# A retention and SwiGLU kernel whose instruction list is made anew: row tiles for the state products, stores on a second queue

## The chip, the cores and the metric

The kernel runs on one core of a Trainium2 chip. Its engines work side by side, each through its own instructions in order: TensorE (PE) multiplies matrices, VectorE (DVE), ScalarE (ACT) and GpSimd (POOL) do elementwise work, and SyncE (SP) issues DMA transfers. The metric is the device time of one execution in microseconds (us), as the median of several runs. Smaller is better.

## The reference

Two parts are chained. The first is a retention recurrence over 4 batches, 8 heads, 768 positions and 64 channels:

```python
gamma = 1.0 - 2.0 ** (-5.0 - np.arange(H))
for t in range(S):
    state = gamma * state + np.einsum('bhd,bhe->bhde', k[:, :, t], v[:, :, t])
    y[:, :, t] = scale * np.einsum('bhd,bhde->bhe', q[:, :, t], state)
```

The second takes y as 3072 rows (tokens) of 512 numbers and applies a normalised feed-forward block with an inner width of 1536:

```python
xn = x / np.sqrt(np.mean(x * x, axis=-1, keepdims=True) + 1e-06) * rms_g
g = xn @ w_gate
out = (g * (1.0 / (1.0 + np.exp(-g))) * (xn @ w_val)) @ w_out
```

## The kernel before, in words

The 768 positions are cut into six chunks of 128 (index c, 0 to 5). A tile is one chunk of one batch, (c, b), 128 tokens. For each tile the scores inside the chunk are computed by a matrix product, masked, and multiplied with v; what came before the chunk is held in a state per batch and head and enters as a second product, q times state. All matrix products are in bf16, with f32 sums in PSUM, which has eight banks.

There are no loops in the program's flow. One long string, ORDER, lists every step by a short name, and the kernel emits the steps in this order. Each engine then works through its own steps in the order of the list, and waits between engines and for buffers are put in from what each step reads and writes. A word of the list reads name.numbers/banks@engine: "/53" gives the PSUM bank or banks that the step writes to, "@D", "@A", "@P", "@S" the engine (DVE, ACT, POOL, SP). A bank may be written anew only when the last reader of its old contents is done. The steps that matter:

- Lq, Lk, Lv load rows of q, k, v; Cq and V scale them to bf16; tq and tk transpose them by DMA on SP (in chunks 0 and 1: Tq and Tk on PE, with the copies Eq and Ek); D scales k by decay.
- A (L401) makes the scores of one or two tiles, heads in pairs: with 64 rows each, two products run in two row tiles of the array. M0 and M1 (L423) mask them on DVE, two instructions a tile.
- Y (L438, L442) multiplies the masked scores of a tile with v, eight matmuls, and adds q times state, four matmuls with 128 rows and 128 columns over two heads each, all in one bank.
- Z (L414) makes the q times state products of a pair of tiles (b, b+1) ahead of that, each head by itself: 16 matmuls of 64 rows and 64 columns in row tiles, even heads in one bank and odd heads in another. After it Y.c.b.2 (L433) adds only the eight score products.
- S (ACT, L455) squares and sums a tile's rows, R (POOL, L465, L467) makes the factor of the normalisation, N (DVE, L479) applies it. After Z the tile's even and odd heads lie in two banks: S and N then take two instructions each (L452, L476), and R adds the two sums first (L464).
- X and XE transpose the normalised rows for the feed-forward part: XE by DMA on SP from chunk 2 on, before that X on PE and XE as a copy.
- K, U and B bring the state from one chunk to the next: products on PE (L525), addition on DVE (L534), cast on POOL (L541).
- g and v (L549) are the gate and value products, four matmuls for each block of 128 of the inner width; s (ACT, L560) is the silu, h (DVE, L568) the product of the two.
- d (L575) is the down-projection of a tile, twelve matmuls of 512 columns, sometimes in two parts. e (L597) does it for the last tile in three column pieces. o copies the result from PSUM (ACT or DVE), and st stores it to memory (L588).
- H (L234) are matmuls without use for the result, in places where PE would wait in the head.

The list before has one Z, for the pair (4,2) and (4,3), and all stores on SP. The buffers in SBUF are rings; six result buffers (o_sb), six scaled q, ten k, and so on, so a load or a copy may also wait for an old buffer's readers.

Of the kernel before, what the change touches and what calls it, by code (L numbers as in the profile page):

```python
# [17 lines left out]
Lk.0.2@S H.4/4 yd causal Lv.0.2@S>causal yt rms.1@S ident Ck.0.2@A Lq.0.0@P H.8/1 Lq.0.1@P Lq.0.2@P Tk.0.2/7 H.2/5  # L18
Lk.0.0@P Tq.0.1/0 vd Tq.0.0/4 Ek.0.2@D Lk.0.1@P Tq.0.2/1 Lk.0.3@P G/7 V.0.2@D Eq.0.1@D Tk.0.0/0 Tk.0.1/6 Eq.0.2@D
Eq.0.0@D iota Lq.0.3@P A.0.2/31 Lv.0.1@P mk0 Lv.0.0@P Lv.0.3@P Ek.0.0@D mk1 GE@A wg.0.2 M1.0.2 wv.0.2 H.2/4 M0.0.2  # L20
Ek.0.1@A A.0.0/5270 D.0.2@P M1.0.1 Tk.0.3/6 Y.0.2/1 Tq.0.3/0 M0.0.1 H.2/4 tab Lk.1.1@P M1.0.0 M0.0.0 S.0.2 Ek.0.3@A
J.0.0/4 J.0.1/7 R.0.2 Y.0.1/2 Eq.0.3@A S.0.1 H.1/6 H.3/0 H.1/5 D.0.0@D Y.0.0/3 N.0.2 J.0.3/5 D.0.1@D wv.2.4 R.0.1
X.0.2/6 N.0.1 S.0.0 wg.2.4 A.0.3/41 R.0.0 X.0.1/0 XE.0.2@A wg.4.6 D.0.3@D M0.0.3 XE.0.1@A g.0.0.2.2.3/2 K.0.2.2/5
K.0.0.2/6 M1.0.3 U.0.2.2@A s.0.0.2.2.3 N.0.0 v.0.0.2.2.3/7 g.0.0.2.1.2/0 h.0.0.2.2.3 Y.0.3/5 Lq.1.0@P wv.4.6 X.0.0/3
U.0.0.2@A S.0.3 wg.6.9 Tk.1.1/4 v.0.0.2.1.2/2 XE.0.0@D s.0.0.2.1.2 h.0.0.2.1.2 g.0.0.2.0.1/6 R.0.3 wv.6.9 Ek.1.1@A
v.0.3.4.0.3/3 v.0.2.3.0.3/4 N.0.3 g.0.3.4.0.3/0 Lk.1.2@P s.0.0.2.0.1 X.0.3/6 v.0.0.2.0.1/5 XE.0.3@A Lk.1.0@P B.0.0
wg.9.12 s.0.3.4.0.3 Lq.1.1@P g.0.5.6.0.3/1 g.0.2.3.0.3/7 h.0.3.4.0.3 s.0.2.3.0.3 Lq.1.2@P h.0.2.3.0.3 g.0.4.5.0.3/0
wv.9.12 h.0.0.2.0.1 s.0.4.5.0.3 v.0.0.4.3.4/2 g.0.0.4.3.4/7 v.0.4.5.0.3/3 mc.1@P s.0.5.6.0.3 s.0.0.4.3.4 h.0.0.4.3.4
wo.0.4 v.0.5.6.0.3/4 h.0.5.6.0.3 D.1.1@P Lv.1.1@P h.0.4.5.0.3 Lv.1.0@P g.0.8.9.0.4/7 g.0.6.7.0.4/0 mc.0@D s.0.8.9.0.4
v.0.4.6.3.4/4 g.0.4.6.3.4/5 s.0.4.6.3.4 v.0.8.9.0.4/6 D.1.0@D D.1.2@P wo.4.8 s.0.6.7.0.4 Tk.1.2/2 Ek.1.2@D Tq.1.0/5  # L30
g.0.7.8.0.4/1 Eq.1.0@D h.0.8.9.0.4 v.0.6.7.0.4/7 h.0.4.6.3.4 wo.8.12 v.0.7.8.0.4/3 s.0.7.8.0.4 h.0.6.7.0.4
g.0.11.12.0.4/5 s.0.11.12.0.4 Tk.1.0/7 h.0.7.8.0.4 Tq.1.1/0 Lv.1.2@P Lq.1.3@P Tq.1.2/3 Eq.1.1@D B.0.1 Eq.1.2@D
g.0.9.10.0.4/4 s.0.9.10.0.4 B.0.2 g.0.10.11.0.4/2 s.0.10.11.0.4 Ek.1.0@D A.1.0/3710 M1.1.1 A.1.2/46 v.0.10.11.0.4/2
v.0.11.12.0.4/0 M0.1.2 M0.1.1 v.0.9.10.0.4/5 M0.1.0 Lv.2.0@S d.0.0.0.4/1 M1.1.0 M1.1.2 h.0.9.10.0.4 Y.1.1/3
d.0.3.0.4/6 Lk.2.3@P h.0.11.12.0.4 Y.1.0/4 S.1.1 Lk.1.3@P R.1.1 h.0.10.11.0.4 S.1.0 N.1.1 d.0.1.0.4/0 R.1.0
d.0.2.0.4/5 N.1.0 X.1.1/3 d.0.2.4.8 d.0.0.4.8 Lv.1.3@P d.0.3.4.8 X.1.0/7 d.0.3.8.12 XE.1.0@A Y.1.2/2 Tq.1.3/7
d.0.0.8.12 S.1.2 d.0.1.4.8 Lq.2.0@S XE.1.1@D o.0.0@A Eq.1.3@D o.0.3@A R.1.2 N.1.2 Tk.1.3/1 d.0.2.8.12 X.1.2/3 Ek.1.3@A
Lk.2.2@P D.1.3@D Lq.2.1@S A.1.3/17 XE.1.2@A M1.1.3 K.1.0/4 K.1.2.2/6 K.1.1/2 B.0.3 M0.1.3 Lq.2.2@S tk.2.2 Lk.2.0@P
g.1.0.1.0.3/3 v.1.2.3.0.3/7 U.1.1@D Y.1.3/1 s.1.0.1.0.3 g.1.1.2.0.3/3 S.1.3 Lk.2.1@P g.1.3.4.0.3/2 o.0.2@A R.1.3
U.1.2.2@D d.0.1.8.12 Cq.2.1@P s.1.3.4.0.3 U.1.0@D g.1.2.3.0.3/2 v.1.0.1.0.3/5 N.1.3 Lq.3.1@S s.1.1.2.0.3 X.1.3/3  # L40
h.1.0.1.0.3 tk.2.0 v.1.3.4.0.3/1 Lk.3.1@P tq.2.1 v.1.1.2.0.3/5 B.1.2 XE.1.3@D h.1.3.4.0.3 s.1.2.3.0.3 h.1.2.3.0.3
# [595 lines left out]
```

## Time and profile before

| | |
|---|---|
| median of 3 runs | 232.84 us (232.34 to 233.55) |
| the profiled execution | 231.99 us |
| its span, first to last instruction | 230.3 us |
| granted TensorE clock | 1.000 |
| PE busy | 224.7 us (98%) |
| DVE, ACT, POOL busy | 127.8, 84.2, 105.7 us |
| HBM read, written | 28.31 MB, 6.29 MB |

The profile is of one execution. Its times are in us from the first instruction. A row of a timeline gives the start, the length, the engine, the line, the operation with output and inputs, how many instructions were put together, and in brackets how long the engine was idle before and what released it. Matmuls overlap a little at their ends, so the length of a PE step is best read from its start to the start of the next one. Rows of groups give the total time and the mean in nanoseconds behind the bar.

### The profile page before, as it was taken

The page shows a single profiled execution, that of the slowest core. Times are in us where ns is not written, and L with a number is a line of the kernel's source. Part 1 is how long each engine was busy: PE and PEld are TensorE (multiplying, and loading weights), DVE is VectorE, ACT ScalarE, POOL GpSimd, SP SyncE. Part 2 cuts the span into 40 slices and gives each one's busy share as a digit, 9 for nine tenths or more (in the row PEclk, how much of TensorE's full clock was granted, in tenths as well). Part 3 has the DMA queues.
Part 4 walks back from the last instruction along what each step waited for, and adds up shares of the span by engine and source line. Part 5 has one row for each costly group of instructions (what it writes and reads, how often), then busy time and mean ns, then how long its engine had stood idle before and what let it go on. Part 6 is the DMA issues. An engine that isn't in the chain of part 4 may idle for free.

```text
span 230.3 us, 4745 instructions
## 1 busy us (share of the span) xinstructions
PE 224.7 (98%) x1849; PEld 118.9 (52%) x1849; DVE 127.8 (55%) x232; ACT 84.2 (37%) x190; POOL 105.7 (46%) x177
## 2 busy tenths in 40 slices
PE   8889999999999999999999999999999999999994
PEld 2568755556564554445544445554554444444552
DVE  5896397936654876477660538756664325432200
ACT  6776524225423340434410435561354124222021
POOL 8979999327879435536269801338040000000000
PEclk9999999999999999999999999999999999999999
DMA  6999999999999957999999999674116200000142
GB/s 130 162 175 134 187 176 191 199 192 134 141 180 164 156 110 180 215 187 228 184 84 288 177 179 271 132 85 90 49 23 198 101 0 0 0 16 35 45 181 92
DMA packets 105352, 31.51 MB, mean 137 GB/s; under 512 B 94449, under 2 KB 102385, under 8 KB 105330
## 3 DMA queue, kind: packets, MB, share of 16 engines
q0 software_dynamic: 40112, 9.70, 45.5%
q1 hardware_dynamic: 65218, 21.51, 43.7%
q8 instruction: 14, 0.23, 0.4%
q14 instruction: 8, 0.07, 0.1%
HBM read 28.31 MB, written 6.29 MB: 150 GB/s over the span
## 4 chain that ended last, share of the span: by engine, by line
PE 93%; DVE 2%; DMA 2%; POOL 1%; issue 0%; ACT 0%; POOLq 0%; DVEq 0%
PE v_ps L549 27%; PE g_ps L549 27%; PE o_ps L575 26%; PE a_ps L401 2%; PE y_ps L438 2%; DMA qb<-in_q_dram 2%; PE y_ps L442 2%; PE kv_ps L525 1%; PE o_ps L597 1%; DVE am L423 1%; PE t_ps L369 1%; PE xt_ps L492 1%; DVE kd L514 1%; PE t_ps L364 1%; POOL qb L307 1%; PE g_row_ps L290 0%
## 5 line engine op out<-in xcount | busy, mean ns | idle before, releaser
L568 DVE TENSOR_TENSOR hT<-sg,v_ps 128x512 bf16<-128x512 bf16 (+2 forms) x76 | 48.0, 656 | 55.4 <-PE v_ps L549 40.2
L560 ACT ACTIVATE sg<-g_ps 128x512 bf16<-128x512 f32 (+2 forms) x76 | 42.3, 575 | 93.6 <-PE g_ps L549 85.2
L549 PE MATMUL g_ps<-xnT,wg_b 128*128 128x512 bf16 (+2 forms) x344 | 71.1, 344 | 0.0
L549 PE MATMUL v_ps<-xnT,wv_b 128*128 128x512 bf16 (+2 forms) x344 | 71.0, 344 | 0.0
L575 PE MATMUL o_ps<-wo_b,hT 128*128 128x512 bf16 x276 | 63.4, 379 | 0.0
L549 PEld LDWEIGHTS <-wg_b 128*128 128x128 bf16 x344 | 30.6, 98 | 29.9 <-issue 0.3
L549 PEld LDWEIGHTS <-wv_b 128*128 128x128 bf16 x344 | 30.5, 98 | 29.1 <-DVE hT L568 0.2
L575 PEld LDWEIGHTS <-hT 128*128 128x128 bf16 x276 | 26.3, 98 | 29.7
L465 POOL TENSOR_SCALAR ms<-ssq 128x1 f32<-128x1 f32 x24 | 4.5, 188 | 42.0 <-ACT xsq L455 41.1
L423 DVE TENSOR_TENSOR am<-a_ps,causal 128x512 bf16<-128x512 f32 x32 | 20.1, 684 | 3.2 <-PE a_ps L401 3.2
L479 DVE SCALAR_TENSOR_TENSOR xn<-y_ps,rstd,g_bc 128x512 bf16<-128x512 f32 x22 | 16.4, 749 | 9.8 <-POOL rstd L467 8.0
L541 POOL CAST st_b<-st_f 64x256 bf16<-64x256 f32 x40 | 18.1, 452 | 5.4 <-DVE st_f L534 4.1
L455 ACT ACTIVATE xsq<-y_ps 128x512 f32<-128x512 f32 x22 | 13.1, 598 | 15.6 <-PE y_ps L442 14.1
L309 POOL DMA_DIRECT2D kb<-in_k_dram x20 | 18.4, 921 | 0.0
L140 ACT COPY o_sb<-o_ps 128x512 f32<-128x512 f32 (+1 forms) x15 | 8.4, 568 | 24.0 <-PE o_ps L575 23.7
L337 POOL TENSOR_TENSOR qb<-qf,ydec 128x512 bf16<-128x512 f32 x13 | 13.9, 1069 | 5.0 <-DMA qf<-in_q_dram 2.3
L467 POOL TENSOR_TENSOR rstd<-ms,mhalf 128x1 f32<-128x1 f32 x24 | 13.3, 555 | 2.0
L140 DVE COPY o_sb<-o_ps 128x512 f32<-128x512 f32 (+2 forms) x11 | 6.7, 622 | 13.3 <-PE o_ps L575 7.6
L356 POOL TENSOR_TENSOR vp<-vf,vdec 128x512 bf16<-128x512 f32 x9 | 9.3, 1046 | 3.7 <-DMA vf<-in_v_dram 3.5
L423 DVE TENSOR_TENSOR am<-a_ps,mask 128x512 bf16<-128x512 f32 x16 | 9.9, 682 | 1.6 <-PE a_ps L401 1.5
L438 PEld LDWEIGHTS <-am 128*128 128x128 bf16 x176 | 7.7, 98 | 3.5
L234 PE MATMUL hot_ps<-one 128*128 128x512 bf16 x23 | 7.9, 491 | 1.1 <-DVE one L147 1.1
(96 smaller groups left out, 158.9 us busy)
## 6 DMA issues: line engine op xcount, KB each, us to landing
out_dram<-o_sb SPq DMA_DIRECT2D x23, 256.0 KB, 2.4
vf<-in_v_dram SPq DMA_DIRECT2D x17, 256.0 KB, 4.1
qf<-in_q_dram SPq DMA_DIRECT2D x16, 256.0 KB, 4.5
kb<-in_k_dram POOLq DMA_DIRECT2D x23, 128.0 KB, 5.4
wo_b<-in_moe_w_out_dram POOLq DMA_DIRECT2D x3, 512.0 KB, 10.3
qb<-in_q_dram POOLq DMA_DIRECT2D x8, 128.0 KB, 5.6
vp<-in_v_dram POOLq DMA_DIRECT2D x7, 128.0 KB, 6.2
wg_b<-in_moe_w_gate_dram POOLq DMA_DIRECT2D x3, 256.0 KB, 5.8
```

What stands on the lines that cost most here:

```text
L140: return (e.copy if e is ACT else e.tensor_copy)(out, in_)
L309: i = done[n, c, b] = e.dma_start(out=x, in_=rows[n][b, c])
L337: e.tensor_tensor(out=u["qb"], in0=u["qf"], in1=ydec[:, c, :, None].to_broadcast([128, H, D]), op=ALU.mult)
L423: return DVE.tensor_tensor(out=u["am"][:, i], in0=u["a"][i], in1=m, op=ALU.mult)
L455: return ACT.activation(xsq, flat(u["y"]), AF.Square, accum_out=u["ssq"])
L467: return POOL.tensor_tensor(out=u["rstd"], in0=ms, in1=mhalf, op=ALU.pow)
L479: return DVE.scalar_tensor_tensor(out=u["xn"], in0=flat(u["y"]), scalar=u["rstd"], in1=g_bc, op0=ALU.mult, op1=ALU.mult)
L541: POOL.tensor_copy(st_b[b][r, :, i * 64:i * 64 + 64], st_f[b // 2][r, b % 2])
L549: r = nc.tensor.matmul(p[:, (n - n0) * m:(n - n0 + 1) * m], W[w][0][:, s, n * 128:(n + 1) * 128], xnT[c][:, s, b0 * C:b1 * C], start=s == ...
L560: return ACT.activation(sg[:, :cols], done["wg", c, n0, b0][:, :cols], AF.Silu)
L568: return DVE.tensor_tensor(out=hT[c][:, n0:n1, b0 * C:b1 * C], in0=sg, in1=p, op=ALU.mult)
L575: nc.tensor.matmul(o_ps[c, b], hT[c][:, n, b * C:(b + 1) * C], wo_b[:, n, :], start=n == 0, stop=n == NFF - 1)
```

## The change

Only the string ORDER differs. The first 202 words are the same steps on the same engines in the same order, up to the last masks before the first down-projection; the banks in them are numbered anew. From there on:

- five more pairs get a Z and the short Y: (2,0), (3,0), (4,0), (5,2) and (5,0), with banks of their own;
- 15 stores are issued by ACT instead of SP;
- the order of all steps, the banks, and the engine of some 30 copies and scalings (o, V, Cq) are new.

The core of the diff, the first words, the beginning of the new part, and two places of the later list:

```diff
 ...
-Lk.0.2@S H.4/4 yd causal Lv.0.2@S>causal yt rms.1@S ident Ck.0.2@A Lq.0.0@P H.8/1 Lq.0.1@P Lq.0.2@P Tk.0.2/7 H.2/5
+Lk.0.2@S H.4/0 yd causal Lv.0.2@S yt rms.1@S ident Ck.0.2@A Lq.0.0@P H.8/1 Lq.0.1@P Lq.0.2@P Tk.0.2/0 H.2/1 Lk.0.0@P
 ...
-K.0.0.2/6 M1.0.3 U.0.2.2@A s.0.0.2.2.3 N.0.0 v.0.0.2.2.3/7 g.0.0.2.1.2/0 h.0.0.2.2.3 Y.0.3/5 Lq.1.0@P wv.4.6 X.0.0/3
+M1.0.3 U.0.2.2@A s.0.0.2.2.3 N.0.0 v.0.0.2.2.3/5 g.0.0.2.1.2/0 h.0.0.2.2.3 Y.0.3/3 Lq.1.0@P wv.4.6 X.0.0/5 U.0.0.2@A
 ...
-v.0.3.4.0.3/3 v.0.2.3.0.3/4 N.0.3 g.0.3.4.0.3/0 Lk.1.2@P s.0.0.2.0.1 X.0.3/6 v.0.0.2.0.1/5 XE.0.3@A Lk.1.0@P B.0.0
+v.0.2.3.0.3/6 N.0.3 g.0.3.4.0.3/3 Lk.1.2@P s.0.0.2.0.1 X.0.3/5 v.0.0.2.0.1/2 XE.0.3@A Lk.1.0@P B.0.0 wg.9.12
 ...
-v.0.4.6.3.4/4 g.0.4.6.3.4/5 s.0.4.6.3.4 v.0.8.9.0.4/6 D.1.0@D D.1.2@P wo.4.8 s.0.6.7.0.4 Tk.1.2/2 Ek.1.2@D Tq.1.0/5
-g.0.7.8.0.4/1 Eq.1.0@D h.0.8.9.0.4 v.0.6.7.0.4/7 h.0.4.6.3.4 wo.8.12 v.0.7.8.0.4/3 s.0.7.8.0.4 h.0.6.7.0.4
+v.0.4.6.3.4/3 g.0.4.6.3.4/6 s.0.4.6.3.4 v.0.8.9.0.4/0 D.1.0@D D.1.2@P wo.4.8 s.0.6.7.0.4 Tk.1.2/6 Ek.1.2@D Tq.1.0/2
+g.0.7.8.0.4/4 Eq.1.0@D h.0.8.9.0.4 v.0.6.7.0.4/6 h.0.4.6.3.4 wo.8.12 v.0.7.8.0.4/0 s.0.7.8.0.4 h.0.6.7.0.4
 ...
+o.2.1@D s.3.8.9.0.4 h.3.8.9.0.4 s.3.0.1.0.4 tq.4.0 A.4.0/3205 Lv.4.2@S h.3.0.1.0.4 Z.4.0/64 M1.4.1 M1.4.0 Lv.4.1@S
+v.3.2.3.0.4/7 st.1.0@A Lv.4.3@S Cq.4.3@P M0.4.0 g.3.2.3.0.4/5 g.3.11.12.0.4/2 g.3.7.8.0.4/3 V.4.0@P M0.4.1 tq.4.3
+Lk.4.2@P s.3.10.11.0.4 tk.4.2 Lq.4.2@S s.3.2.3.0.4 V.4.3@D st.1.3@S Lk.4.3@P Y.4.0.2 s.3.11.12.0.4 v.3.10.11.0.4/2
+S.4.0 V.4.2@A Cq.4.2@D V.4.1@D h.3.2.3.0.4 d.2.2.0.12/5 h.3.10.11.0.4 R.4.0 N.4.0 tk.4.3 Lq.5.2@S tq.4.2 A.4.2/2701
 ...
-o.5.1@A st.4.2@S o.5.3.1@D d.5.2.0.12/0 st.5.3.2@S st.5.1@S st.5.3.1@S e.5.3.0/1 o.5.2@A st.5.2@S o.5.3.0@A st.5.3.0@S
+o.5.0@A o.5.1@A st.5.0@A o.5.2@A st.4.0@S st.5.1@S o.5.3.1@A st.5.2@S e.5.3.0/5 st.5.3.2@A o.5.3.0@A st.5.3.0@A
+st.5.3.1@S
```

134 lines of the change are left out of this document (65 added, 69 removed).

## The prediction

> **What bounds the kernel now.** I read the page first, then the waits of TensorE's own queue, then the timelines of TensorE (PE) and VectorE (DVE) side by side.
>
> ```profile
> span 230.3 us, 4745 instructions
> PE 224.7 (98%) x1849; PEld 118.9 (52%) x1849; DVE 127.8 (55%) x232; ACT 84.2 (37%) x190; POOL 105.7 (46%) x177
> PE 93%; DVE 2%; DMA 2%; POOL 1%; issue 0%; ACT 0%; POOLq 0%; DVEq 0%
> ```
>
> ```profile
> PE hot_ps L234 <- DVE one L147: 1.1, 1, 1.1
> PE t_ps L364 <- DMA qb<-in_q_dram: 0.5, 1, 0.5
> PE xt_ps L492 <- DVE xn L479: 0.4, 1, 0.4
> PE t_ps L364 <- DVE am L423: 0.2, 1, 0.2
> ```
>
> PE is the bound. The four waits above are all that it has, 2.2 us, and the last of them lies at 17 us. From there to its last product the matmuls stand shoulder to shoulder. So the change can win only matmul time, and can lose wherever a new order or a new bank makes PE wait. There is little to gain and much room to lose.
>
> **The state products as row tiles.** Five pairs are new (pair 4.2 had it already). Rows from PE's timeline; a step lasts from its start to the start of the next:
>
> ```profile
> 78.33 0.39 PE L442 MATMUL y_ps<-st_b,qT 128*128 128x128 bf16 x4
> 78.64 0.44 PE L525 MATMUL kv_ps<-vp,kb 128*64 128x64 bf16 x16
> 79.02 0.62 PE L401 MATMUL a_ps<-qT,kT 64*128 64x128 bf16 x16
> ...
> 82.40 0.39 PE L442 MATMUL y_ps<-st_b,qT 128*128 128x128 bf16 x4
> 82.63 0.40 PE L438 MATMUL y_ps<-vp,am 128*128 128x64 bf16 x8
> ...
> 148.67 0.41 PE L414 MATMUL y_ps<-st_b,qT 64*128 64x64 bf16 x16
> 149.01 1.04 PE L549 MATMUL v_ps<-xnT,wv_b 128*128 128x512 bf16 x4
> ```
>
> The state part of one tile is 0.23 us (82.40 to 82.63), of a pair 0.46; the 16 row tiles of a pair take 0.34 (148.67 to 149.01). That saves 0.12 us a pair, 0.6 for five. Going from whole-array matmuls to tiles costs something too: after the four of 78.33 (0.23) the kv products begin at 78.64, 0.08 late, while kv to a_ps has no such gap. Counted through both lists there are 18 such entries before and 20 after, so 0.16 goes back. Net: -0.4 us. [...] The pair measured here shows 0.46 against 0.34, a factor of 1.35, and I take the row. [...]
>
> What the row tiles add elsewhere: each of ten tiles gets two squares, two accumulator reads, two normalisations and an addition.
>
> ```profile
> L455 ACT ACTIVATE xsq<-y_ps 128x512 f32<-128x512 f32 x22 | 13.1, 598 | 15.6 <-PE y_ps L442 14.1 <-PE y_ps L438 1.3
> L455 ACT ACTIVATION_READ_ACCUMULATOR xsq<-y_ps 128x1 f32 x22 | 4.4, 199 | 0.0
> L452 ACT ACTIVATE xsq<-y_ps 128x256 f32<-128x256 f32 x4 | 1.5, 392 | 0.0
> L452 ACT ACTIVATION_READ_ACCUMULATOR xsq<-y_ps 128x1 f32 x4 | 0.9, 219 | 0.0
> L476 DVE SCALAR_TENSOR_TENSOR xn<-y_ps,rstd,g_bc 128x256 bf16<-128x256 f32 x4 | 1.8, 480 | 2.1 <-POOL rstd L467 2.1
> L464 POOL TENSOR_TENSOR ssq<-ssq 128x1 f32<-128x1 f32 x2 | 0.4, 192 | 7.1 <-ACT xsq L452 7.1
> ```
>
> ACT: 2 x (392 + 219) - (598 + 199) = 0.43 us a tile; POOL 0.19; DVE 2 x 480 less one whole normalisation (0.74 in a row below) = 0.22. The way from a tile's scores to its transposed rows gets 0.84 us longer. Cover: by PE's steps in the new list 7 to 10 us of matmuls stand between the last scores of a chunk and the first gate product that reads them. If that cover were gone, PE would pay up to 0.84 once a chunk, for four chunks; I take 0.
>
> **The banks of the head.** The list's first 202 words are the same, but the numbers behind the slashes (PSUM banks) are not. A matmul that takes a bank waits until the last reader of what lay in it is done. So each new pair of reader and taker is to be checked at the times of the old run. Most pass. These do not:
>
> ```profile
> 18.62 0.74 DVE L479 SCALAR_TENSOR_TENSOR xn<-y_ps,rstd,g_bc 128x512 bf16<-128x512 f32 x1
> 19.28 0.41 DVE L568 TENSOR_TENSOR hT<-sg,v_ps 128x256 bf16<-128x256 bf16 x1
> ...
> 21.92 0.75 DVE L479 SCALAR_TENSOR_TENSOR xn<-y_ps,rstd,g_bc 128x512 bf16<-128x512 f32 x1 [0.74 <-POOL rstd L467]
> ```
>
> ```profile
> 19.27 0.40 PE L438 MATMUL y_ps<-vp,am 128*128 128x64 bf16 x8
> 19.51 0.39 PE L492 MATMUL xt_ps<-ident,xn 128*128 128x128 bf16 x4
> ...
> 22.17 0.81 PE L549 MATMUL g_ps<-xnT,wg_b 128*128 128x384 bf16 x4
> 22.82 0.39 PE L492 MATMUL xt_ps<-ident,xn 128*128 128x128 bf16 x4
> ```
>
> Y.0.3 (PE at 19.27) gets bank 3, which N.0.0 still reads until 19.36; X.0.0 (19.51) gets bank 5, which h.0.0.2.2.3 reads until 19.69. PE loses about 0.2 us. Then g.0.3.4.0.3 (22.17) gets bank 3 from Y.0.3, which N.0.3 reads from 21.92 to 22.67. N.0.3 waits for a POOL instruction (rstd), not for PE, so it comes no later than before; the product starts at 22.67 + 0.06 = 22.73, +0.56 in all, the first 0.2 included. The 0.06 is from a vector end to the matmul that waited for it, as here (16.16 + 0.75 = 16.91, then 16.97):
>
> ```profile
> 16.16 0.75 DVE L479 SCALAR_TENSOR_TENSOR xn<-y_ps,rstd,g_bc 128x512 bf16<-128x512 f32 x1
> ...
> 16.97 0.40 PE L492 MATMUL xt_ps<-ident,xn 128*128 128x128 bf16 x4 [0.40 <-DVE xn L479]
> ```
>
> Later DVE is behind because of a mask and a decay product:
>
> ```profile
> 29.81 2.20 DVE L276 TENSOR_TENSOR mask<-causal,vdec 128x512 f32<-128x512 bf16 x1
> 31.94 1.52 DVE L514 TENSOR_TENSOR kd<-kb,vdec 128x512 bf16<-128x512 bf16 x1
> 33.39 0.41 DVE L140 COPY kT<-t_ps 128x512 bf16<-128x512 bf16 x1
> 33.72 0.67 DVE L378 TENSOR_TENSOR qT<-t_ps,qdec 128x512 bf16<-128x512 bf16 x1
> 34.32 2.20 DVE L568 TENSOR_TENSOR hT<-sg,v_ps 128x512 bf16<-128x512 bf16 x4
> ```
>
> ```profile
> 33.47 1.89 PE L549 MATMUL v_ps<-xnT,wv_b 128*128 128x512 bf16 x8
> ```
>
> v.0.6.7.0.4 (the first four of 33.47) gets bank 6, which the copy Ek.1.2 reads until 33.80: it starts at 33.86, +0.39. v.0.7.8.0.4 would follow at 34.72 (four matmuls are half of the step that ends at 35.20) and gets bank 0, which h.0.8.9.0.4, the first of the four at 34.32, reads until about 34.95: +0.29. DVE's chain there starts from PE's own products, so it moves with the earlier 0.56 and the waits add up: 0.56 + 0.39 + 0.29 = 1.24 us. Bounds: 0, if DVE comes earlier than the old rows by the 0.4 to 0.7 at stake, and 1.5, if the mask again takes its longest. I take 1.2, the rows' own value.
>
> **The rest of the list made anew.** I laid the PE steps of the new list end to end and looked, for each step, at who must be done before it. Most have as much room as their like in the old list. The tightest is A.4.2, which reads qT of 4.2: the load, Cq.4.2 (now DVE) and the transposing DMA stand late, behind four other DMAs on SP (load, store, transpose, load).
>
> ```profile
> 138.04 0.62 PE L401 MATMUL a_ps<-qT,kT 64*128 64x128 bf16 x16
> ...
> 138.50 2.47 DVE L423 TENSOR_TENSOR am<-a_ps,causal 128x512 bf16<-128x512 f32 x4
> 140.90 0.68 DVE L337 TENSOR_TENSOR qb<-qf,ydec 128x512 bf16<-128x512 f32 x1
> ...
> DMA to landing us min/median/max: 2.4/4.7/8.3
> ```
>
> (the last row is the transposing DMAs of qT.) In the new list DVE does after A.4.0 four masks, V.4.3 and Cq.4.2: 0.46 to the first mask, 2.47, twice 0.68, together 4.3 us after A.4.0's start. The landing is 6.7, 9.0 or 12.6 us after it. PE has until A.4.2: scores 0.55, tiles 0.34, five ffn steps of 0.86 (half of 33.47 to 35.20), Y 0.24, twelve down matmuls 2.6 (at 0.216), the entry 0.08: 8.1 us. So A.4.2 waits 0, 0.9 or 4.5 us. I take 0.4: the low end is that of a quiet queue, and loads for chunk 5 are under way then. Some ten other steps come out within 0.1 us of their releaser (M1.1.3 behind o.0.0 now on DVE, h.3.7.8 behind N.4.1, M1.5.3 behind two V products); for all of them 0.2, from 0 to 1. What queues behind a waiting DVE or SP instruction there is the next mask or transpose, so one miss feeds the next.
>
> **Stores on ScalarE.** No store on ACT is in the trace. The nearest row:
>
> ```profile
> L588 SPq DMA_DIRECT2D out_dram<-o_sb x10: 332/332/442, 206.2 to 227.5; - x10
> ```
>
> Fifteen at 0.33 are 5 us, on an engine that is 37% busy. Where one stands ahead of an activation that PE waits for, it can cost its 0.33; taken off SP it can bring nothing, since PE waits for nothing of SP in the old run. I take 0, with 0 to 1 for three such places. At the end the last product takes the bank of o.5.2 after one product of 1.0 us, and that copy (0.59) fits; the last copy and its store are as before. 0.
>
> **Sum.** -0.4 + 1.2 + 0.4 + 0.2 = +1.4 us on the profiled execution (231.99 us with 230.3 of span): 233.4. The median of the runs, 232.84, lies 0.85 above that execution, so I forecast 234.3 us (+0.6%). About 0.5%, 1.2 us, is what a measurement of this kernel can tell from no change.
>
> **Rivals.** (1) Not slower: the head's banks cost nothing, because DVE reaches N.0.3, Ek.1.2 and h.0.8.9 earlier. For it: four numbers decide, each within 0.7 us. Against: DVE's order and inputs in the head are unchanged. It decides from a DVE lead of 0.7 us at 34 us. Then -0.4 + 0.6 = +0.2: 233.0. (2) Transposes on SP become the bound: at 8.3 us of landing A.4.2 waits 4.5, and 1.4 - 0.4 + 4.5 gives 238.3; with half of that, 236. For it: loads and transposes share SP's queue in a new order; against: the transposes before it on SP are due earlier, and a landing up to 3.8 us costs nothing. [...] (4) The row tiles are not there: excluded, since PE's instruction list grows by 80, five times 32 added less 16 removed.
>
> **Chances.** Forecast with both head waits, 233.6 to 235.4: 0.50; rival 1, 232.4 to 233.6: 0.31; rival 2, above 235.4: 0.15; rival 3: 0.04. The range 232.4 to 237.0 leaves out rival 3 and the upper part of rival 2. Slower by over 0.5% (above 234.0): the larger part of the forecast's case and all of rival 2, 0.56; within: 0.40; faster: 0.04.
>
> **What would show it.** Waits of PE for DVE near 19, 22 and 33 to 35 us, and the first down matmuls 1.2 us later than in the old run; L414 at 96 instead of 16 with 0.34 a pair; from there to the last matmul about as long as in the old run. The forecast is wrong if the first down matmul comes when it did, or if PE waits over 1 us anywhere behind it.

## The result: 0.4% slower, by waits that the forecast had only in part

The changed kernel takes 233.31 us (median of 20 runs, 232.19 to 234.40); the kernel before, in 20 runs beside it, 232.37 us. The ratio is 1.0040, 95% interval 1.0027 to 1.0054. (The ratios here and below leave out the few executions that were far slower than the rest, and are not the quotient of two medians.) The forecast was 234.3 us: the direction held and the time lies in the range, but the effect, +0.94 us, is two thirds of the +1.46 forecast, and the median of three runs on which it stood (232.84) was itself 0.47 too high.

The page of the changed kernel: the span, the busy times, and the chain that ended last by engine.

```profile
span 231.5 us, 4820 instructions
...
PE 222.5 (96%) x1863; PEld 117.8 (51%) x1889; DVE 129.2 (56%) x244; ACT 87.5 (38%) x220; POOL 101.3 (44%) x182
...
PE 79%; DMA 9%; POOL 6%; DVE 2%; issue 2%; ACT 1%; SPq 0%; POOLq 0%; DVEq 0%
```

The span is 1.2 us longer (230.3 before). In the chain DMA has 9% where it had 2%, and POOL 6% where it had 1%. PE is still the bound, and these shares are not the loss by themselves: g3 below, which is faster than the changed kernel, has 9% and 6% too. The waits of PE's queue (who waited for whom; us in total, times, longest):

```profile
PE t_ps L365 <- DMA qb<-in_q_dram: 1.3, 1, 1.3
PE hot_ps L235 <- DVE one L148: 1.1, 1, 1.1
PE a_ps L402 <- DVE am L424: 0.6, 1, 0.6
PE v_ps L550 <- DVE kT L141: 0.6, 1, 0.6
PE xt_ps L493 <- DVE xn L480: 0.5, 1, 0.5
PE v_ps L550 <- DVE hT L569: 0.2, 1, 0.2
PE v_ps L550 <- issue: 0.2, 1, 0.2
PE o_ps L576 <- DMA xnT<-xn: 0.2, 1, 0.2
```

The last two rows (0.2 us) are not waits: this trace lacks 26 matmul records (1863 for 1889 weight loads), and both rows stand where one is lacking. Before, nothing stood in this list behind 17 us. Now there are three kinds: the loads of q in the head (1.3 for 0.5), the copies at 34 to 36 us (kT, hT: the banks of the forecast), and, new, masks at 168 us (am). The timelines of PE and of DVE at the second kind:

```profile
33.13 1.03 PE L550 MATMUL g_ps<-xnT,wg_b 128*128 128x512 bf16 x4
34.71 1.02 PE L550 MATMUL v_ps<-xnT,wv_b 128*128 128x512 bf16 x4 [0.55 <-DVE kT L141]
35.90 1.02 PE L550 MATMUL v_ps<-xnT,wv_b 128*128 128x512 bf16 x4 [0.17 <-DVE hT L569]
```

```profile
32.77 1.56 DVE L515 TENSOR_TENSOR kd<-kb,vdec 128x512 bf16<-128x512 bf16 x1 [0.62 <-DMA kb<-in_k_dram]
34.25 0.41 DVE L141 COPY kT<-t_ps 128x512 bf16<-128x512 bf16 x1
```

The product v.0.6.7.0.4 takes the bank that the copy kT (Ek.1.2) reads, as forecast. But the copy is late because the decay product kd before it waited for a load of k, and then took 1.56 us. The third kind, with DVE, SP (the issue of loads and transposes) and PE:

```profile
164.99 0.68 DVE L357 TENSOR_TENSOR vp<-vf,vdec 128x512 bf16<-128x512 f32 x1
165.59 0.68 DVE L569 TENSOR_TENSOR hT<-sg,v_ps 128x512 bf16<-128x512 bf16 x1
167.01 0.69 DVE L357 TENSOR_TENSOR vp<-vf,vdec 128x512 bf16<-128x512 f32 x1 [0.75 <-DMA vf<-in_v_dram]
167.62 0.68 DVE L424 TENSOR_TENSOR am<-a_ps,causal 128x512 bf16<-128x512 f32 x1
```

```profile
161.60 1.91 SPq L386 DMA_TRANSPOSE qT<-qb  x1
163.57 0.57 SPq L310 DMA_DIRECT2D vf<-in_v_dram  x1
```

```profile
167.39 0.41 PE L415 MATMUL y_ps<-st_b,qT 64*128 64x64 bf16 x16
168.36 0.62 PE L402 MATMUL a_ps<-qT,kT 64*128 64x128 bf16 x16 [0.56 <-DVE am L424]
```

The load of v of (5,2) is issued at 163.57, behind a transpose. DVE, with its scaling V.5.2 next in the queue, is idle for 0.75 us until it lands and the scaling begins at 167.01. The mask M1.5.3, whose scores had been there since 163, stands behind the scaling, and A.5.0 needs the mask's bank. DVE takes the two in the order of the list: the mask begins only at 167.62, as the scaling ends (167.70).

By places: the first down matmul comes at 43.50 (41.99 before), 1.51 us later; from it to PE's last product it is 184.87 us (185.11 before), 0.24 shorter. Of the 1.51 us, 0.35 is there when X.0.1 begins (17.32 for 16.97), 0.33 is lost from there to g.0.3.4.0.3, 1.04 at 34 to 36 us, and 0.2 comes back between and behind these. The 0.33 us are in no list of waits; the starts in PE's timeline show them:

```profile
17.32 0.40 PE L493 MATMUL xt_ps<-ident,xn 128*128 128x128 bf16 x4 [0.53 <-DVE xn L480]
...
19.77 0.39 PE L439 MATMUL y_ps<-vp,am 128*128 128x64 bf16 x8
20.09 0.38 PE L493 MATMUL xt_ps<-ident,xn 128*128 128x128 bf16 x4
...
22.85 0.81 PE L550 MATMUL g_ps<-xnT,wg_b 128*128 128x384 bf16 x4
```

Y.0.3 comes 2.45 us behind X.0.1 (2.30 before), X.0.0 2.77 (2.54), g.0.3.4.0.3 5.53 (5.20). Each starts 0.04 to 0.06 us behind the end of the reader that the forecast named (N.0.0 at 19.72, h.0.0.2.2.3 at 20.05, N.0.3 at 22.79). So the new banks do cost something here, 0.33 us where the forecast had 0.56.

### The profile page after: what moved, and what is told of

Its sections match the earlier page's. It is cut to its first block, busy times and chain, and to the rows that moved or that the text cites. A ratio compares the mean times of both kernels' runs of the same rounds, so it can differ in the third digit from the quotient of the medians.

```text
span 231.5 us, 4820 instructions
## 1 busy us (share of the span) xinstructions
PE 222.5 (96%) x1863; PEld 117.8 (51%) x1889; DVE 129.2 (56%) x244; ACT 87.5 (38%) x220; POOL 101.3 (44%) x182
## 4 chain that ended last, share of the span: by engine, by line
PE 79%; DMA 9%; POOL 6%; DVE 2%; issue 2%; ACT 1%; SPq 0%; POOLq 0%; DVEq 0%
PE v_ps L550 24%; PE o_ps L576 23%; PE g_ps L550 22%; DMA kb<-in_k_dram 4%; PE a_ps L402 3%; DMA qb<-in_q_dram 2%; PE y_ps L434 2%; DMA vf<-in_v_dram 1%; POOL rstd L468 1%; PE o_ps L598 1%; DMA xnT<-xn 1%; POOL wg_b L322 1%; PE y_ps L439 1%; PE kv_ps L526 1%; PE t_ps L365 1%
## 5 line engine op out<-in xcount | busy, mean ns | idle before, releaser
L576 PE MATMUL o_ps<-wo_b,hT 128*128 128x512 bf16 x265 | 61.4, 379 | 0.7 <-DMA xnT<-xn 0.2
L542 POOL CAST st_b<-st_f 64x256 bf16<-64x256 f32 x40 | 16.7, 418 | 6.6 <-DVE st_f L535 5.1
L338 POOL TENSOR_TENSOR qb<-qf,ydec 128x512 bf16<-128x512 f32 x10 | 10.4, 1039 | 17.1 <-DMA qf<-in_q_dram 17.0
L465 POOL TENSOR_TENSOR ssq<-ssq 128x1 f32<-128x1 f32 x12 | 2.3, 191 | 35.2 <-ACT xsq L453 35.1
L141 ACT COPY o_sb<-o_ps 128x512 f32<-128x512 f32 (+2 forms) x16 | 8.4, 533 | 23.1 <-PE o_ps L576 17.2
L480 DVE SCALAR_TENSOR_TENSOR xn<-y_ps,rstd,g_bc 128x512 bf16<-128x512 f32 x12 | 9.0, 747 | 10.3 <-POOL rstd L468 10.3
L453 ACT ACTIVATE xsq<-y_ps 128x256 f32<-128x256 f32 x24 | 8.9, 382 | 13.5 <-PE y_ps L434 13.5
L456 ACT ACTIVATE xsq<-y_ps 128x512 f32<-128x512 f32 x12 | 7.1, 596 | 15.8 <-PE y_ps L443 14.6
L477 DVE SCALAR_TENSOR_TENSOR xn<-y_ps,rstd,g_bc 128x256 bf16<-128x256 f32 x24 | 10.5, 477 | 3.5 <-POOL rstd L468 1.9
L357 POOL TENSOR_TENSOR vp<-vf,vdec 128x512 bf16<-128x512 f32 x7 | 7.5, 1071 | 5.1 <-DMA vf<-in_v_dram 5.1
```

Of the source, the lines that this page charges most:

```text
L338: e.tensor_tensor(out=u["qb"], in0=u["qf"], in1=ydec[:, c, :, None].to_broadcast([128, H, D]), op=ALU.mult)
L453: ACT.activation(xsq[:, i * 256:i * 256 + 256], flat(u["ys"][i]), AF.Square, accum_out=u["ssq"][:, i:i + 1])
L477: DVE.scalar_tensor_tensor(out=x[:, :, i], in0=u["ys"][i], scalar=u["rstd"], in1=g[:, :, i], op0=ALU.mult, op1=ALU.mult)
L480: return DVE.scalar_tensor_tensor(out=u["xn"], in0=flat(u["y"]), scalar=u["rstd"], in1=g_bc, op0=ALU.mult, op1=ALU.mult)
L542: POOL.tensor_copy(st_b[b][r, :, i * 64:i * 64 + 64], st_f[b // 2][r, b % 2])
L576: nc.tensor.matmul(o_ps[c, b], hT[c][:, n, b * C:(b + 1) * C], wo_b[:, n, :], start=n == 0, stop=n == NFF - 1)
```

## The experiments

Each kernel differs in the order list alone. In the diffs, words of the list stand without their surroundings. "Before" is the median of the kernel before, run beside it; the ratio has its 95% interval. Each kernel of the table below the first ran 12 times, i1 8 and g1 6 times. The column "first d" is the start of the first down matmul in the profiled execution, "body" the time from there to PE's last product.

| kernel | us | before | ratio (interval) | first d | body |
|---|---|---|---|---|---|
| the changed kernel | 233.31 | 232.37 | 1.0040 (1.0027 to 1.0054) | 43.50 | 184.87 |
| e1_head | 234.14 | 232.26 | 1.0080 (1.0056 to 1.0103) | 41.66 | 187.18 |
| e2_gate | 232.65 | 232.26 | 1.0012 (0.9992 to 1.0033) | 42.24 | 185.21 |
| e3_whole | 233.52 | 232.26 | 1.0051 (1.0032 to 1.0070) | 43.31 | 185.93 |
| e4_apart | 232.67 | 232.26 | 1.0017 (0.9999 to 1.0035) | 42.78 | 185.45 |
| f1_head | 233.66 | 232.39 | 1.0043 (1.0020 to 1.0066) | 42.78 | 186.34 |
| f2_headonly | 232.16 | 232.39 | 0.9992 (0.9971 to 1.0014) | 42.04 | 185.08 |
| f3_nogate | 232.52 | 232.39 | 0.9997 (0.9971 to 1.0023) | 43.81 | 185.11 |
| f4_again | 233.37 | 232.39 | 1.0030 (1.0006 to 1.0055) | 42.99 | 185.16 |
| g1_stores_sp | 235.34 | 232.14 | 1.0121 (1.0078 to 1.0165) | 41.54 | 186.37 |
| g2_stores_act | 233.08 | 232.14 | 1.0050 (1.0024 to 1.0077) | 41.92 | 185.76 |
| g3_scale_pool | 231.97 | 232.14 | 0.9979 (0.9959 to 0.9999) | 41.92 | 184.91 |
| g4_repaired | 232.07 | 232.14 | 1.0001 (0.9978 to 1.0025) | 41.86 | 184.54 |
| h1_after | 233.03 | 232.27 | 1.0047 (1.0022 to 1.0072) | 44.10 | 184.92 |
| h2_scale_again | 232.09 | 232.27 | 0.9980 (0.9963 to 0.9997) | 42.04 | 184.27 |
| h4_loads | 232.33 | 232.27 | 1.0003 (0.9980 to 1.0026) | 42.35 | 184.95 |
| h3_more | 232.19 | 232.27 | 0.9990 (0.9963 to 1.0018) | 42.21 | 184.51 |
| i1_whole | 233.87 | 232.35 | 1.0055 (1.0029 to 1.0081) | 42.99 | 185.88 |
| i2_apart | 232.62 | 232.35 | 1.0023 (1.0000 to 1.0045) | 43.47 | 185.69 |

**First theory: the head's banks.** The first trace seemed to confirm the forecast: 1.5 us lost ahead of the first down-projection. The rival was an edit that the forecast had passed over: the first load of v (Lv.0.2) no longer waits for the causal mask (the word ">causal" in the first line of the diff).

e1_head: the banks of the kernel before in the first 202 words, the body's banks permuted to follow.

```diff
-Tk.0.2/0 H.2/1 ... v.0.6.7.0.4/6 v.0.7.8.0.4/0 ...
+Tk.0.2/7 H.2/5 ... v.0.6.7.0.4/7 v.0.7.8.0.4/3 ...
```

> The changed kernel with the banks of the kernel before in the first 202 words (the banks behind them renamed among themselves so that they fit); the released first load of v stays released. Theory B (the head's new banks cost the time): the waits of TensorE near 34.7 and 35.9 us and the delays near 19.8 and 22.8 go, 1.2 us in all; the first down-projection moves from 43.5 to about 42.3 us and the whole is 1.2 us shorter than the changed kernel, 0.2 to 0.3 us under the kernel before. Rival L (the load that is no longer ordered behind the causal mask delays the loads of q in the head, and the rest follows from that lateness): the first down-projection stays at 43.3 to 43.5 us and the time within 0.3 us of the changed kernel.

Its first down matmul came at 41.66, as theory B has it, yet the kernel was slower than the changed one. The permutation made new pairs at the joint; PE's waits have

```profile
PE o_ps L576 <- DVE am L424: 1.3, 1, 1.3
...
PE a_ps L402 <- ACT sg L561: 0.9, 1, 0.9
```

The first comes of the permutation (d.0.0.0.4 takes the bank of the mask M1.1.2). The second does not: it is A.3.2 at 107 us, in a body whose order had not been touched. So the run decides nothing on the head, and points elsewhere.

e2_gate: one word.

```diff
-Lv.0.2@S
+Lv.0.2@S>causal
```

> The changed kernel with the one word put back that orders the first load of v behind the causal mask. Theory L: TensorE's wait for the loads of q falls from 1.3 to 0.5 us, TensorE is 0.35 us earlier at 17 us, and the first down-projection and the whole come 0.35 us earlier (if the later waits only follow the lateness, up to 1.2 us). Theory B: the waits for the old readers of the banks stay, 1.1 to 1.2 us from 19 to 36 us; at most the 0.35 us of the loads comes back, or nothing if the loads scatter by that much from one execution to the next.

The ratio, 1.0012, lies between that of the kernel before and that of the changed one; the wait for q was 0.7. Not decided by this run alone.

e3_whole and e4_apart: the five new pairs back to whole products; the row tiles of two pairs away from the score products.

```diff
-Z.3.0/40 ... Y.3.0.2 ... Y.3.1.2
+Y.3.0/4 ... Y.3.1/0
```

> The changed kernel with the five new pairs of row tiles taken back to whole products, tile by tile, on the same banks; order, engines and stores are those of the changed kernel. Theory of the forecast (a pair of row tiles takes 0.34 us wherever it stands): 0.4 to 0.6 us slower than the changed kernel. Theory S (a tile step beside another tile step shares its entry and exit, so that such a pair adds only 0.24 us): 0.9 us slower, 0.22 us a pair where the pair stood beside the score products and next to nothing for the pair (5,0), which stands alone. Rival N (row tiles are worth nothing, the later normalisation gives it back): within 0.2 us.

```diff
-A.3.0/7512 ... Z.3.0/40 d.1.0.0.10/6
+A.3.0/7512 ... d.1.0.0.10/6 Z.3.0/40
```

> The changed kernel with the row tiles of the pairs (3,0) and (4,0) moved behind the next product on TensorE, so that they no longer stand beside the score products. Theory S: score products and row tiles each pay an entry of 0.09 us and an exit of 0.10 us of their own, 0.19 us a pair, 0.4 us for the two; in the trace the score products go from 0.45 to 0.55 us and 0.09 us appears ahead of the row tiles, which themselves stay at 0.34. Theory of the forecast (an entry only): 0.08 us a pair, 0.16 for the two. Rival: no difference, if the entry is no price of the row tiles but a wait for scores or queries.

The intervals overlap that of the changed kernel (e4 came out below it, against both theories). Something that differs from one execution to the next is as large as the effects. Both were repeated later on quieter ground (i1, i2).

**Head or body.** f1_head has the head of the kernel before, word for word, and the changed body with its banks renamed so that the joint keeps its pairs; f2_headonly is the reverse, the old body behind the head's new banks; f3_nogate is the kernel before without ">causal"; f4_again is the changed kernel.

```diff
-(first 202 words of the changed kernel) A.2.0/6053 ... d.2.1.0.10/5 ...
+(first 202 words of the kernel before)  A.2.0/7241 ... d.2.1.0.10/4 ...
```

> The head (first 202 words) of the kernel before, with its banks and its ordered load of v, and behind it the body of the changed kernel with its banks renamed one to one (banks 0 to 7 become 2, 6, 3, 1, 0, 4, 7, 5), so that the copies and masks at the joint meet the same readers as in the changed kernel. Theory H (all of the loss lies in the head): the first down-projection at 42.0 us as before, no wait of TensorE from 17 us to it, and the time under that of the kernel before by the 0.24 us by which the body was shorter in the first profile of the changed kernel, down to 0.9 us under it where the wait ahead of the second score products of chunk 5 stays away. Rival J (the new body is slower by itself, through its waits for masks and loads): 0.2 us or more above the kernel before.

```diff
-(kernel before) Tk.0.2/7 H.2/5 ... v.0.6.7.0.4/7 v.0.7.8.0.4/3 ...
+(f2_headonly)   Tk.0.2/0 H.2/1 ... v.0.6.7.0.4/6 v.0.7.8.0.4/0 ...
```

> The kernel before with only the banks of its head taken from the changed kernel (the load of v stays ordered behind the mask; the banks of the body are renamed one to one). Theory B (the head's new banks cost the time by themselves): 0.6 to 1.2 us slower than the kernel before, with waits of TensorE at 34 to 36 us. Theory BL (the banks cost something only where a load is late, since the wait at 34 us comes from a vector product that waits for a load of k): 0.2 us slower at 19 to 23 us, and between 0 and 1 us more from one execution to the next, so that the runs scatter wider than those of the kernel before.

```diff
-Lv.0.2@S>causal
+Lv.0.2@S
```

> The kernel before with one word less: the first load of v no longer waits for the causal mask. Theory L: TensorE waits longer for the loads of q in the head (0.5 us in the profile before, 1.3 in that of the changed kernel), and all that follows comes 0.35 to 0.7 us later; the time is 0.3 to 0.7 us above the kernel before. Rival (the load costs nothing, the loads of q scatter by that much anyway): within 0.2 us.

> The changed kernel once more, beside the three others on one chip, to see how much its waits differ between two profiled executions. Theory BL: the wait for the copy of k near 34 us is present when the vector engine's product before it had to wait for a load, absent when not; between the two executions the first down-projection moves by up to 1 us. Theory B: the waits are there in each execution at the same length within 0.2 us. In both the time is 0.9 us above the kernel before, within 0.4.

By the medians this speaks against the first theory. The head's new banks with the old body cost nothing that 12 runs can tell (0.9992; the interval is -0.7 to +0.3 us), nor does the released load (0.9997), and the old head with the new body costs as much as the whole change (1.0043). The banks and the released load together, on the old body, were not run.

The traces say more than the medians. From X.0.1 to g.0.3.4.0.3 PE takes 5.20 us in all five profiles with the old banks and 5.52 to 5.53 in the twelve with the new ones in which no load of weights holds it up there: 0.32 us is a fixed price. The wait for kT at 34 us comes and goes. It was there in f4 (0.71), and absent in f2, e2 and e4; over all profiles with the new banks it is there in 5 of 15 (0.3 to 1.0 us). Theory BL was half right: in those five kd waited 0.43 us or more for its load of k and also took 1.16 us or more; in the ten others it waited 0.26 us at most, or took 0.69.

The body of f1 shows another mechanism. DVE, ACT and PE of f1 near 106 us:

```profile
105.21 0.69 DVE L357 TENSOR_TENSOR vp<-vf,vdec 128x512 bf16<-128x512 f32 x1 [2.97 <-DMA vf<-in_v_dram]
105.82 1.28 DVE L569 TENSOR_TENSOR hT<-sg,v_ps 128x512 bf16<-128x512 bf16 x2
```

```profile
106.59 0.60 ACT L561 ACTIVATE sg<-g_ps 128x512 bf16<-128x512 f32 x1 [1.66 <-DVE hT L569]
```

```profile
107.24 0.62 PE L402 MATMUL a_ps<-qT,kT 64*128 64x128 bf16 x16 [0.56 <-ACT sg L561]
```

and the same scaling in the changed kernel:

```profile
103.91 0.69 DVE L357 TENSOR_TENSOR vp<-vf,vdec 128x512 bf16<-128x512 f32 x1 [1.80 <-DMA vf<-in_v_dram]
```

V.3.2 on DVE waits 3.0 us for its load; two gate multiplications stand behind it; ACT waits for a buffer that they free; the gate product's bank and with it A.3.2 wait for ACT. In the changed kernel's first profile the same wait was 1.8 us and used up the slack without reaching PE. Behind 42 us DVE waits for loads of v 2.5 us in the changed kernel, 3.4 in f1; the kernel before has no such row.

**Theory V: loads that come late, under scalings on VectorE.** Rival Q: the stores on ScalarE.

g1_stores_sp and g2_stores_act: the 15 stores back to SP, and the same 15 of the kernel before to ScalarE.

```diff
-st.0.2@A st.1.1@A ... st.5.3.0@A
+st.0.2@S st.1.1@S ... st.5.3.0@S
```

> The changed kernel with its 15 stores of ScalarE given back to SP, at the same places in the list. Theory Q (the stores on a queue of their own do harm, by the extra queue of DMAs from the start on or in front of activations): 0.5 to 1.0 us faster than the changed kernel. Theory V (the loss lies in loads that come late: vector products that scale v stand in VectorE's queue and wait for a load issued late on SP): SP has 15 times 0.6 us more to issue, some of it ahead of loads, so the same or up to 0.5 us slower. The forecast's term (nothing either way): within 0.2 us.

> The kernel before with the same 15 stores issued by ScalarE. Theory Q: 0.5 to 1.0 us slower than the kernel before. The forecast's term: ScalarE is 37 percent busy, TensorE waits for none of it, within 0.2 us of the kernel before.

g1 is the slowest of all, 1.2% above the kernel before, about 2 us slower than the changed kernel. In its trace DVE waits 3.2 us for loads of v (2.5 in the changed kernel). Its waits have

```profile
PE t_ps L370 <- DVE xn L480: 1.0, 1, 1.0
...
PE a_ps L402 <- DVE am L424: 0.5, 1, 0.5
```

The first of these is at 53 us and stands in e2 and g3 too (0.6 and 0.5); only the second is V's. The profiled execution is the fastest of the six (233.19 us), so its trace doesn't show where the 2 us lie. The run is against Q. It is on V's side, but V had expected 0.5 us at most. g2 is 0.5% slower than the kernel before, as Q had it and the forecast had not: stores on ScalarE are not free in the old list, and their price there, 0.9 us by the medians, is as large as the whole loss. One wait is new in its trace, 0.5 us for transposed rows. What the store has to do with that is not settled.

g3_scale_pool: three scalings on GpSimd, nothing else.

```diff
-V.3.2@D ... V.5.3@D ... V.5.2@D
+V.3.2@P ... V.5.3@P ... V.5.2@P
```

> The changed kernel with three scalings of v, those of (3,2), (5,2) and (5,3), on GpSimd instead of VectorE; nothing else moves. Theory V: VectorE no longer stands idle for loads of v (2.2 to 3.4 us in the profiles so far), the masks behind them come 0.7 us or more earlier, the wait of the score products of (5,0) and (5,1) near 168 us (0.6 us in two of three profiles of the changed kernel) goes and that of the score products near 106 us cannot come: 0.5 us faster than the changed kernel, within 0.2. Rival H (the loss lies ahead of the first down-projection): no faster than 0.2 us, since the waits in the body are then a small part.

231.97 us, a ratio of 0.9979 to the kernel before. Against the medians beside them that is 1.1 us better than the changed kernel, twice what V had expected (0.5).

g4_repaired: these three, ">causal" put back, and U.2.1 and B.2.1 ahead of U.2.2.2.

```diff
-U.2.2.2@D XE.2.2@S B.2.0 ... A.3.0/7512 U.2.1@D o.1.3@A B.2.1
+U.2.1@D U.2.2.2@D XE.2.2@S B.2.0 B.2.1 ... A.3.0/7512 o.1.3@A
```

> The changed kernel with the three scalings on GpSimd, the word put back that orders the first load of v behind the mask, and the state sum and copy of (2,1) moved ahead of those of (2,2) and (2,3), so that the row tiles of (3,0) need not wait for it. If theory V and the interplay of load order and banks in the head are the two parts of the loss: 0.7 us less by the word (as in the run with it alone), 0.5 by the scalings, 0.1 to 0.3 by the copy: 232.0 to 231.6 us, 0.4 to 0.8 under the kernel before; no wait of TensorE over 0.3 us behind 17 us. If the body is slower for another reason: 232.6 us or more.

Expected 231.6 to 232.0, measured 232.07: the word and the copy gave nothing more.

**The same on one chip, and what makes the loads late.** h1 is the changed kernel and h2 the three scalings again; h4_loads keeps the scalings on VectorE and issues two loads of v earlier; h3_more adds to h2 the copy of g4 and a shift in chunk 1.

> The changed kernel again, on the same chip as the next three. Theory V (late loads under vector products): 0.9 us above the kernel before, within 0.4, with VectorE idle 2 us or more for loads of v behind 42 us and TensorE waiting 0.4 us or more for masks or activations there. Rival H (the loss lies ahead of the first down-projection): the first down-projection at 42.8 us or later, the body of this execution no longer than that of the kernel before.

> The three scalings of v on GpSimd once more, beside the changed kernel on one chip. Theory V: 0.6 to 1.4 us faster than the changed kernel, at or under the kernel before. Rival C (the earlier difference came from the chips): within 0.3 us of the changed kernel.

```diff
-tk.3.2 R.3.0 ... Cq.3.3@P ... tq.3.3 ... Lv.3.2@S
+Lv.3.2@S tk.3.2 R.3.0 ... Cq.3.3@P ... tq.3.3
-Lv.5.3@S ... tq.5.1 M1.5.2 Lv.5.2@S
+Lv.5.3@S Lv.5.2@S ... tq.5.1 M1.5.2
```

> The changed kernel with two loads of v issued earlier on SP and nothing else: that of (3,2) three transposes earlier, that of (5,2) one transpose earlier; the scalings stay on VectorE. Theory V: VectorE waits at most 0.5 us for loads of v behind 42 us, and the gain is that of the three moved scalings, 0.6 to 1.4 us, less up to 0.3 for the transposes that now come 0.6 us later. Rival W (the gain of the moved scalings came from taking 1.8 us of work off VectorE): within 0.3 us of the changed kernel.

```diff
-Tq.1.3/0 ... Tk.1.3/7 X.1.1/4 X.1.0/2 d.0.1.8.12
+Tq.1.3/0 d.0.1.8.12 ... Tk.1.3/7 X.1.1/4 X.1.0/2
```

> The three scalings on GpSimd, the state sum and copy of (2,1) ahead of those of (2,2) and (2,3), and in chunk 1 a third of a down-projection moved ahead of the transposes of k of tile (1,3), with the copy of the third result tile ahead of the first rows, so that the bank of these transposes need not be waited for (0.3 to 0.8 us at 52 us in three profiles). Theory V with all waits gone: the saving of the row tiles stands alone, 231.3 to 231.8 us, 0.6 us or more under the kernel before. If the move only shifts the wait to the score products of (1,3): 231.9 to 232.1, as with the scalings alone.

The scalings gave 0.94 us against the changed kernel on this chip (233.03 to 232.09), and two loads issued earlier gave 0.70 with all the work still on VectorE (the intervals of h1 and h4 just touch; h2 and h4 can't be told apart). So it is mainly the lateness, not VectorE's load. In h2 the place at 166 us reads, on DVE and PE:

```profile
164.11 0.69 DVE L569 TENSOR_TENSOR hT<-sg,v_ps 128x512 bf16<-128x512 bf16 x1 [0.46 <-ACT sg L561]
164.71 0.68 DVE L424 TENSOR_TENSOR am<-a_ps,causal 128x512 bf16<-128x512 f32 x1
```

```profile
165.97 0.41 PE L415 MATMUL y_ps<-st_b,qT 64*128 64x64 bf16 x16
166.21 0.72 PE L402 MATMUL a_ps<-qT,kT 64*128 64x128 bf16 x16
```

The mask follows the multiplication at once, ends 0.8 us before A.5.0, and the score products follow the row tiles without a wait. In h4 DVE has no wait for a load of v either:

```profile
165.51 0.69 DVE L357 TENSOR_TENSOR vp<-vf,vdec 128x512 bf16<-128x512 f32 x1
166.11 0.69 DVE L424 TENSOR_TENSOR am<-a_ps,causal 128x512 bf16<-128x512 f32 x1
```

h3 gave nothing over h2.

The profiles bear this out in part. In all nine with the new body as the list had it (the changed kernel three times, e1 to e4, f1, g1), A.5.0 waits 0.1 to 0.7 us for the mask or A.3.2 waits 0.6 to 0.9 for ScalarE; in none of the seven with the scalings moved or the loads issued earlier (g3, g4, h2, h3, h4, i1, i2) does either wait so. That is 0.5 us a profile, about half of the loss. The other half the rows do not place. Between the profiles of the changed kernel and those of g3 and h2 most of the difference lies ahead of the first down matmul (42.99 to 44.10 us for 41.92 and 42.04), where these edits change nothing; the body is 184.87 to 185.16 us for 184.91 and 184.27. The profile of h1 by itself has the signs of rival H as well as those of theory V: 44.10 us, and a body no longer than before. Five profiles can't tell whether that is chance. It is the medians of f1, g3, h2 and h4 that put the loss into the body.

**What the row tiles give.** On the version of h2:

> The version with the three scalings of v on GpSimd, and the five new pairs of row tiles taken back to whole products on the same banks. Theory S (tile steps that stand together share entry and exit): 0.8 to 0.9 us slower than with the row tiles, so 0.4 to 0.7 above the kernel before. The forecast's term: 0.4 us slower than with the row tiles, so level with the kernel before within 0.3.

> The version with the three scalings of v on GpSimd, and the row tiles of the pairs (3,0) and (4,0) moved behind the next product, away from the score products. Theory S: 0.4 us slower than beside them (0.19 a pair), in the trace 0.09 ahead of and 0.10 behind each. The forecast's term (an entry of 0.08 only): 0.2 us slower. If (3,0) had waited for the copied state where it stood, up to 0.3 of that comes back.

The rows of PE in i1 and in h2 for the scores of (2,2), (2,3) and the first tile of pair (2,0):

```profile
79.31 0.62 PE L402 MATMUL a_ps<-qT,kT 64*128 64x128 bf16 x16
79.87 0.41 PE L439 MATMUL y_ps<-vp,am 128*128 128x64 bf16 x8
80.11 0.39 PE L443 MATMUL y_ps<-st_b,qT 128*128 128x128 bf16 x4
80.33 2.32 PE L576 MATMUL o_ps<-wo_b,hT 128*128 128x512 bf16 x10
```

```profile
78.25 0.62 PE L402 MATMUL a_ps<-qT,kT 64*128 64x128 bf16 x16
78.70 0.40 PE L415 MATMUL y_ps<-st_b,qT 64*128 64x64 bf16 x16
79.03 0.41 PE L434 MATMUL y_ps<-vp,am 128*128 128x64 bf16 x8
79.28 2.11 PE L576 MATMUL o_ps<-wo_b,hT 128*128 128x512 bf16 x9
```

Scores that are followed by a whole product take 0.56; followed by row tiles, 0.45. So a pair beside scores adds 0.33 - 0.11 = 0.22 where two whole state products add 0.45 (0.22 for the one shown, 80.11 to 80.33, and 0.23 as in the forecast's rows for the other). Moved away from the scores (i2), they pay for themselves again:

```profile
136.38 0.62 PE L402 MATMUL a_ps<-qT,kT 64*128 64x128 bf16 x16
136.94 1.04 PE L550 MATMUL v_ps<-xnT,wv_b 128*128 128x512 bf16 x4
137.91 0.41 PE L415 MATMUL y_ps<-st_b,qT 64*128 64x64 bf16 x16
138.25 1.04 PE L550 MATMUL g_ps<-xnT,wg_b 128*128 128x512 bf16 x4
```

0.56 for the scores, 0.97 for the product between (0.10 over its 0.87), 0.34 for the tiles: 0.2 us more than beside the scores. i2 was 0.5 us above h2 (0.4 expected; in other runs). In i1 the body is 1.61 us longer than in h2 (185.88 and 184.27); 0.86 of it is the pitch, from start to start, of the score, state and kv products (16.44 for 15.58 us in sum), as theory S had it. The rest, 0.75, lies in the other steps; 0.3 of it shows as waits, such as 0.2 us for queries ahead of A.5.0. By the medians i1 lies 1.5 us above the kernel before and h2 0.2 below, 1.7 where 0.8 to 0.9 was expected; the double is not explained.

## Why the prediction was right in sign and wrong in its steps

On the profiled execution the sum came out almost exactly, +1.35 us for +1.4 (233.34 and 231.99), and its largest term too: the head's banks cost 0.33 + 1.04 = 1.37 us there for the 1.24 of the forecast. That is chance. In two further executions of the same list the second part was 1.20 and 0.10 us, and by the medians the change costs 0.94.

- **Row tiles, -0.4: mis-sized, -0.85.** The body without waits is 184.27 (h2) for 185.11; the other profile of the same list, g3, has 184.91 with one wait of 0.46 in it. The saving is twice the forecast's. The step that failed is to price a pair at 0.34 wherever it stands, with an entry each. The list puts three of the five right behind score products and one right ahead of them, where entry and exit are shared (scores of 0.45 us for 0.56 in the rows of h2 and i1). There a pair adds 0.22 for 0.45, with the 0.11 saved on the scores counted in: a factor of two, where the forecast took 1.35 from the one pair that it had. Tiles that stand away from the scores lose 0.2 us of it again in i2, 0.1 behind the scores and 0.1 ahead of the tiles; what takes that time is not shown.
- **The normalisation hidden, 0: right.** Behind 17 us PE waits for no normalisation in h2, with the tiles in place. In five other profiles (e2, f1, g1, g3, g4) it waits 0.2 to 1.0 us for one at 53 us, but that is in chunk 1, which has no row tiles of the state product.
- **Head banks, +1.2: a third of it is fixed, the rest failed.** The pairs of reader and taker were read rightly. Of the 0.56 us at 19 to 23 us, 0.32 is there in all twelve profiles with the new banks in which weights came in time. Of the 0.68 at 34 to 36 us nothing is fixed: the two steps there lose 0 to 1.5 us, next to nothing in seven of the 15 profiles. The step that failed is "DVE's order and inputs in the head are unchanged", from which a fixed time was read out of one execution: one input is a load of k that can come late, and the product that reads it took from 0.68 to 1.56 us. In g3 DVE reads

```profile
32.06 0.69 DVE L515 TENSOR_TENSOR kd<-kb,vdec 128x512 bf16<-128x512 bf16 x1 [0.47 <-DMA kb<-in_k_dram]
32.67 0.42 DVE L141 COPY kT<-t_ps 128x512 bf16<-128x512 bf16 x1
```

  and PE does not wait at 34 us, with the same banks and a load that is 0.47 us late: the product took 0.69, and the copy ends at 33.09, 0.7 us earlier than in the run that the forecast read. Rival 1 had this: "a DVE lead of 0.7 us at 34 us". But the banks do not cost nothing, as it said: 0.32 stays. The medians of f2 are too coarse to show that.
- **A.4.2 behind a late transpose, +0.4: 0.** In no profile does it wait; rival 2 is out.
- **The rest of the list, +0.2: here was the loss, about 0.9 by the medians** (h1 to h2), of which the rows show about 0.5 as waits. The one place was on the list ("M1.5.3 behind two V products"), the other (V.3.2 at 104 to 105 us) was not. The step that failed: the check went by PE's steps and by the work in DVE's queue, and took loads as there when wanted. The load of v of (5,2) is issued 3.4 us before its scaling and takes as long to land (163.57 to 166.99). Ahead of it SP spends 1.91 us on a transpose; in h4, where the load is issued before that, DVE does not wait for it.
- **Stores, 0:** not decided. In the new list the kernel is about 2 us slower without them on ScalarE (g1); in the old one they cost 0.5% (g2). That they carry no part of the loss is not shown.
- **An edit not priced:** ">causal" was overlooked. By itself it is worth nothing that the runs can tell (f3); together with the new banks it was not tried on the old body.
- **The base:** three runs gave 232.84, twenty 232.37. A profiled execution 0.85 below the median of three was a warning that three are few.

## What to carry to other kernels

An operation that waits for a load holds up what stands behind it in its engine's queue (here 0.75 us on DVE for a load of v, and 0.56 us on PE for the mask behind the scaling), so when a list is made anew, look for each load at the distance from its issue (behind what else is on that queue) to the first operation that needs it, and put operations under late loads on an engine that nobody waits for. A wait read out of one trace need not be a fixed cost. Here the one at 19 to 23 us was the same in all twelve profiles in which no load came late there; the one at 34 us, with a load and a product of varying length in its chain, was a chance. And a repair found that way can be worth the whole change: with three scalings moved to GpSimd the new list is 0.2% faster than the kernel before (0.9980, 0.9963 to 0.9997, and 0.9979, 0.9959 to 0.9999 on another chip; by the medians 0.1%). It is the one version whose interval lies below 1, and only just.

## What was not expected of the hardware

Three executions of the same list reach the first down-projection up to 1.1 us apart (42.99, 43.50 and 44.10 us; the last at a granted clock of 0.993). At X.0.1 they are already 1.75 us apart (16.67 to 18.42), and the two steps at 34 to 36 us then lose 0.1 to 1.2 us; why this scatters isn't settled. The same decay product kd on VectorE took 0.69 us in one execution and 1.56 in another, a difference larger than the wait of 0.55 us that followed the slower one.
